# The same operations in an order searched over 48 replays with scattered landings in place of 16

## The chip, the cores and the metric

The kernel runs on one core of a Trainium2 chip. A core has five engines with a stream of instructions each: TensorE (PE in the profile; PEld is its weight loads), VectorE (DVE), ScalarE (ACT), GpSimd (POOL) and SyncE (SP), which here only issues transfers. POOL issues transfers too, the ones that add into their destination. The metric is device time in microseconds (us), less is better. Each engine works through its own stream in the order written, and the streams meet only at semaphores.

## The reference

For x of 2048 rows and 512 columns the reference computes

```
xn = layernorm(x)
q, k, v = split(xn @ wqkv)                  # 32 heads of 16
pq, pk = phi(q), phi(k)                     # phi(t) = (t + 1 if t > 0 else exp(t)) + 1e-6
o = pq @ (pk^T v) / (pq . sum(pk) + 1e-6)   # by head, no softmax
s = o @ wo
h = gelu(layernorm(xn) @ w1), its four column groups shifted by +1, -1, +2, -2 rows
x1 = xn + h @ w2
m = x1 + gelu(layernorm(x1) @ w3) @ w4      # 512 -> 1376 -> 512
out = x + s * silu(m)
```

## The kernel before

**Products.** Every float32 operand of a product is split into two pieces of the type fp32r, hi (a rounded copy, written by ACT or DVE) and lo (the residual full - hi, a DVE subtraction). A product is then three matmuls: hi by hi, hi by lo, lo by hi (`products`). In the tile names of the profile the last letter says which piece it is: `u_1h` and `u_1l` are the two pieces of `u_1`. Many products go by a scheme with seven block products for eight (`seven`, and `pair_kq` for keys and queries), in which a bank of PSUM takes a first product, is copied out by ACT, and then takes a second product on top.

**Stages in order of time.** Keys and queries of the 16 row tiles of 128 rows, with the gram matrix of x and the keys (`k`, `q`, `pax`, `pbx`, `pex`, `g` in the profile, 4 to 130 us); the row mixer with w1 and w2 (`h`, `pam`, `pbm`, `pem`, to 230); the MLP's first layer, block by block, with the attention products between (`pa`, `pb`, `pe`, `pas`, `pbs`, `pes`; for the first block also the second layer, `acc`, to about 405); the MLP's second layer of the other three blocks (`pad`, `pbd`, `ped`, to 492).

**The start.** Four 128-row chunks of the key weights (`wk_s0` to `wk_s3`) and of the transposed x (`xt0_0` to `xt0_3`, each in two halves) are loaded by SP in an order written out by hand. Four banks `k0` to `k3` take the keys of the first four row tiles, chunk by chunk; `k0` and `k1` take chunk 0 as plain float32 (`k<-wk_s,xt`). DVE sums the weights' chunks (`wkt`, three additions), a float32 product with ones (`ksum`) makes column sums of it, and `feature_k` turns a closed bank of keys into features: DVE `kt` (which needs ksum), ACT, DVE `kr`, ACT `k0h`. The first gram products (`g`) need `k0h` and the normalized x of the tile (`x0h`). The same sum for the query weights is `wqt` and `qsum`.

**What sets the order.** The body of the kernel issues nothing: it adds 5560 operations to a plan, each with its engine, an estimate of its duration and what it depends on. The operations are numbered in the order in which they are added. `Plan.emit` then runs a replay of the chip: again and again it takes, over all engines, the operation that can start first, and issues it, so that the order in which each engine's stream is written comes out of the replay. Among the operations of an engine that could start at about the same moment (within 0.02 us for PE, 0.25 us for the others) the one with the earliest due time goes. A PE operation's due time is its place in the list of matmuls; another operation's follows back from the matmuls that need it. A matmul may not run more than 9 us of products ahead of the first matmul still open (`window`). Products into one bank keep their order within that bank, since each depends on the one before it.

**The table.** Before the replay, `nudged` moves the due times of single operations by a table of pairs, number and k:

```
for n, k in zip(table[::2], table[1::2]):
    self.ops[n].due -= .25 * k
self.backward()
```

A positive k makes an operation due earlier by k quarters of a microsecond, a negative one later. `backward` then makes everything that is not a matmul due in time for those that need it, so a later due time of such an operation holds only where all of its users are later too. The loads of the start have due times 20 us apart in the order written by hand (`in_turn`), far ahead of all other.

Operations that the prediction speaks of, by number: 25 is the residual `u_1l` of the first half of chunk 1 (DVE); 26 the load of the first half of `xt0_2` (SP); 27 the copy `u_2h` of it (ACT); 98 the float32 product of chunk 0 into k1 (PE); 105 to 107 the three products of chunk 1 into k0 (106 is the one with `wk_1l`, 107 the one with `u_1l`); 108 to 110 the same into k1; 122 the last product into k1; 123 to 125 the additions of `wkt` (124 takes in `wk_s2`), 126 the product `ksum`; 174 the load of `wq_s0`; 3568 to 3573 the six products into the bank `pas` of the attention of row tiles 6 and 7; 3581 ACT's copy `p5s` of its bank `pes`; 3589 to 3594 the second product onto that bank.

Of the kernel before, what the change touches and what calls it, by code (L numbers as in the profile page):

```python
# [411 lines left out]
def linear_attn_gated_by_mixer(  # L412
# [1401 lines left out]
    for b in LINE:  # L1814
# [14 lines left out]
        25, 43, 34, 17, 48, 11, 52, 22, 57, 4, 63, 3, 76, 3, 88, -164, 90, 14, 91, -77, 94, 30, 95, 2, 96, 3,  # L1829
        97, 30, 98, -40, 100, -16, 103, 30, 105, -42, 112, 38, 115, -66, 118, -34, 124, 73, 125, 16, 129, 1,  # L1830
        147, 3, 150, 6, 151, -80, 176, 20, 207, 16, 216, 3, 233, 11, 234, 29, 248, 17, 252, 3, 259, 25, 261, 42,
        262, 18, 275, 8, 282, -131, 283, -49, 302, 83, 314, -14, 315, 24, 316, 21, 321, 25, 326, 6, 331, 17,
        336, -29, 341, -44, 354, 27, 355, -45, 375, 27, 405, -6, 406, -36, 410, -76, 415, 40, 416, -23, 424, 11,
        427, 23, 428, -30, 433, -9, 434, -77, 435, 22, 443, 67, 445, -24, 451, 7, 454, -24, 456, 18, 478, 13,
        485, -8, 488, -69, 489, -119, 491, -65, 492, -3, 504, 30, 522, 77, 532, -9, 542, -1, 544, 5, 545, 15,
        552, 36, 553, -28, 563, -29, 568, -26, 571, -22, 586, 29, 591, 24, 600, -25, 616, 11, 618, 10, 627, -50,
        631, 22, 650, 6, 654, -53, 657, -29, 660, 9, 676, 8, 678, 7, 688, -19, 694, -22, 704, -15, 705, 19, 710,
        -18, 713, 22, 714, 15, 717, -23, 721, -22, 724, 36, 726, -14, 728, 7, 733, 5, 761, 17, 797, 13, 806, 36,
        807, -10, 814, -15, 815, -38, 827, 85, 844, 20, 847, 3, 849, -51, 862, -35, 867, -36, 870, -19, 873, 31,
        874, -15, 876, -28, 885, 36, 894, 15, 899, 37, 901, -27, 909, 5, 911, 2, 917, 23, 925, 7, 927, -30, 934,  # L1840
        13, 941, -10, 956, -44, 969, 6, 971, -6, 976, -52, 980, -10, 997, 25, 998, -27, 1000, -24, 1005, -17,
        1013, -11, 1024, -19, 1030, -28, 1082, 6, 1087, -28, 1090, -3, 1101, 39, 1103, -27, 1119, 1, 1141, 13,
        1146, 44, 1149, 20, 1153, 9, 1156, 8, 1177, 27, 1179, 67, 1208, -23, 1213, 4, 1227, -38, 1239, -20,
        1262, 21, 1266, 8, 1271, 44, 1277, 35, 1291, 3, 1323, -12, 1324, -6, 1328, -1, 1329, 29, 1330, -16,
        1331, 19, 1333, -8, 1340, -40, 1362, -46, 1367, 18, 1381, 45, 1389, -46, 1399, -12, 1407, 24, 1408, 22,
        1412, 23, 1416, 13, 1419, 24, 1420, -43, 1421, -8, 1436, 8, 1447, 40, 1470, 42, 1474, -49, 1482, 33,
        1489, -12, 1502, -15, 1517, -42, 1521, -8, 1532, -28, 1540, -40, 1563, -18, 1575, 24, 1584, 20, 1588, 8,
        1596, -19, 1613, 37, 1614, 4, 1619, 33, 1620, 15, 1629, -4, 1631, -3, 1641, -35, 1648, 22, 1652, 49,
        1655, 4, 1659, 15, 1661, -4, 1665, -111, 1677, 11, 1679, -11, 1687, -19, 1696, 32, 1699, -20, 1700, 106,
        1703, -55, 1705, -12, 1717, -75, 1724, 10, 1725, 10, 1726, 15, 1741, 12, 1742, 28, 1747, 35, 1749, 12,  # L1850
        1758, 30, 1771, 17, 1779, -149, 1796, -30, 1843, 16, 1845, 18, 1853, -23, 1854, -28, 1855, -4, 1861,
        -22, 1864, 17, 1866, 31, 1881, -67, 1888, -54, 1901, 61, 1925, -37, 1933, -5, 1938, -86, 1943, 43, 1944,
        -6, 1947, 29, 1951, -16, 1955, -38, 1960, -57, 1964, 57, 1972, 19, 1978, 3, 1985, 4, 1990, -28, 1994,
        -42, 1996, -20, 1999, -38, 2000, 20, 2002, -22, 2008, 28, 2011, -25, 2021, 30, 2029, -31, 2048, -15,
        2049, -4, 2050, -3, 2060, 19, 2063, 43, 2067, 12, 2071, 19, 2080, 3, 2084, 22, 2102, 18, 2104, -26,
        2106, -32, 2112, -20, 2119, 24, 2131, -20, 2156, -24, 2158, 7, 2161, -34, 2190, -5, 2213, 12, 2244, 14,
        2258, 2, 2264, 71, 2267, 21, 2270, 19, 2286, -22, 2295, 5, 2298, -50, 2317, 33, 2326, 9, 2340, 14, 2353,
        12, 2357, 31, 2358, -19, 2381, -52, 2382, 1, 2383, 6, 2387, -14, 2389, -27, 2391, -30, 2393, -3, 2394,
        -15, 2406, 32, 2413, 22, 2422, -6, 2423, 26, 2424, -4, 2446, -16, 2452, 2, 2469, 9, 2471, 24, 2476, 31,
        2478, -18, 2482, 16, 2521, -26, 2534, -11, 2543, 24, 2578, -18, 2580, -14, 2585, 21, 2586, -7, 2592, -9,  # L1860
        2610, 16, 2611, 28, 2622, 21, 2626, 6, 2628, -27, 2639, 31, 2644, -22, 2648, 33, 2649, -8, 2656, -13,
        2658, 24, 2672, 29, 2684, -22, 2690, -4, 2691, -19, 2705, -23, 2710, 6, 2718, 6, 2722, -28, 2724, -47,
        2734, 26, 2739, 28, 2751, 44, 2778, 29, 2792, 17, 2804, 3, 2806, -46, 2816, -32, 2822, 20, 2831, -28,
        2833, 13, 2843, 6, 2855, 8, 2859, 52, 2870, 18, 2872, 8, 2875, 17, 2882, 33, 2892, -26, 2895, -23, 2899,
        -32, 2900, 16, 2904, -33, 2907, -13, 2912, 21, 2919, -24, 2926, 10, 2932, 4, 2935, -17, 2936, -40, 2941,
        -40, 2957, -40, 2963, -90, 2966, -48, 2967, -29, 2978, -20, 2980, 30, 2992, 14, 3029, -22, 3032, 9,
        3034, 36, 3055, 30, 3057, -6, 3061, -10, 3072, 62, 3085, 47, 3091, 25, 3094, 8, 3103, 7, 3124, 97, 3140,
        8, 3146, -6, 3156, -16, 3163, 24, 3204, 104, 3210, -44, 3222, -21, 3229, -63, 3239, -51, 3243, -24,
        3274, 55, 3276, 31, 3287, 41, 3288, 25, 3292, 22, 3311, -22, 3314, -18, 3315, -53, 3316, 21, 3319, -77,
        3321, -18, 3327, 2, 3328, -49, 3330, -52, 3347, 12, 3348, 25, 3374, 14, 3380, 18, 3386, 13, 3406, 28,  # L1870
        3407, -30, 3447, -19, 3450, 33, 3454, -46, 3458, 39, 3466, 50, 3469, -18, 3475, -27, 3480, 9, 3484, 35,
        3486, 106, 3490, -26, 3501, -40, 3509, 37, 3516, 10, 3541, 26, 3557, 4, 3559, 5, 3560, 3, 3561, 22,
        3562, 33, 3563, -30, 3570, 17, 3571, 56, 3584, -15, 3608, -28, 3611, 26, 3621, -42, 3626, 4, 3634, -6,
        3646, -38, 3669, 6, 3672, -26, 3676, -26, 3711, -20, 3721, 10, 3723, 5, 3739, 1, 3768, -3, 3776, 2,
        3777, 2, 3783, -4, 3791, -19, 3796, 7, 3813, -17, 3821, 23, 3826, -31, 3829, -38, 3846, -16, 3863, 11,
        3871, 6, 3878, 2, 3882, -23, 3885, -29, 3894, 61, 3897, -18, 3916, -7, 3926, -26, 3974, 6, 3987, 8,
# [59 lines left out]
```

## Time and profile before

| | |
|---|---|
| time, median of 3 runs | 498.06 us (498.03 to 498.6) |
| the profiled execution's own time | 498.08 us |
| its span, first to last instruction | 496.4 us |
| PE busy | 490.6 us, 99% of the span, 3244 instructions |
| PEld busy | 447.0 us, 90% |
| DVE busy | 438.4 us, 88% |
| ACT busy | 373.4 us, 75% |
| POOL busy | 123.6 us, 25% |
| granted TensorE clock, mean | 0.999 |
| moved by DMA | 117.44 MB, 237 GB/s |

A matmul instruction is on the row of PE from its start until its result is out, so rows of neighbouring matmuls overlap: what PE loses is read from the distance between starts, not from gaps between rows. A line of the timeline has the start, the time taken, engine, line, operation, out<-in, the shapes; in brackets the idle time before it and what ended that. A float32 product stands in the trace as two instructions (x2). SPq and POOLq are the queues that issue transfers.

### The profile page before, as it was taken

To read this page: it belongs to the slowest core of one execution; us is meant where nothing else is said; L and a number is where in the kernel's file an instruction comes from. 1 tells how busy PE (TensorE), PEld (TensorE's weight loads), DVE (VectorE), ACT (ScalarE), POOL (GpSimd) and SP (SyncE) were. 2 spreads that over 40 slices of the span, in tenths; PEclk is the share of its full clock that TensorE was granted. 3 is DMA by queue.
4 is the path that set the end of the run, shared out by engine and by line. 5 is a ranking of instruction groups with operands and counts; after the bars stand their busy time and mean duration, and the time that the engine had idled before them with its cause. 6 is when DMAs were issued, how large, how long until landed. Compare 5 with 4: busy or idle time off the path is not lost.

```text
span 496.4 us, 9885 instructions
## 1 busy us (share of the span) xinstructions
PE 490.6 (99%) x3244; PEld 447.0 (90%) x3244; DVE 438.4 (88%) x874; ACT 373.4 (75%) x845; POOL 123.6 (25%) x214
## 2 busy tenths in 40 slices
PE   8999999999999999999999999999999999999996
PEld 6778888888888999899889999999999999999996
DVE  5998997889989669999999999999999899796864
ACT  5999999677887599999988567765686877565531
POOL 1384404276930232133200021100000000143420
PEclk9999999999999999999999999999999999999999
DMA  7869696999974999999988499984634699599996
GB/s 229 303 187 297 133 296 183 237 287 269 329 220 100 236 310 248 273 252 290 337 268 247 158 194 298 247 262 138 183 114 147 215 336 332 114 226 283 278 224 182
DMA packets 87082, 117.44 MB, mean 237 GB/s; under 512 B 10328, under 2 KB 39160, under 8 KB 87032
## 3 DMA queue, kind: packets, MB, share of 16 engines
q1 hardware_dynamic: 75512, 96.11, 59.6%
q0 software_dynamic: 11520, 20.71, 24.9%
q8 instruction: 25, 0.41, 0.4%
q14 instruction: 25, 0.20, 0.1%
HBM read 72.66 MB, written 39.93 MB: 227 GB/s over the span
## 4 chain that ended last, share of the span: by engine, by line
PE 97%; DMA 1%; SPq 1%; ACT 0%; DVE 0%; issue 0%; ACTq 0%
PE pb L146 12%; PE pbd L146 9%; PE h L146 9%; PE g L146 9%; PE acc L146 6%; PE pe L146 6%; PE pbx L146 6%; PE ped L146 5%; PE pbm L146 5%; PE pbs L146 5%; PE q L146 3%; PE pa L146 3%; PE pex L146 3%; PE k L146 3%; PE pad L146 3%; PE pes L146 2%
## 5 line engine op out<-in xcount | busy, mean ns | idle before, releaser
L225 POOL DMA_DIRECT2D xo<-x1d x12 | 10.9, 950 | 166.2 <-DVE xo L191 118.5
L225 POOL DMA_DIRECT2D th<-in_x x14 | 12.2, 895 | 45.0 <-DVE th L201 23.1
L225 POOL DMA_DIRECT2D o<-xnd x16 | 14.0, 887 | 37.5 <-DVE o L191 13.5
L168 ACT ACTIVATE th<-xo 128x512 f32<-128x512 f32 (+1 forms) x16 | 9.7, 614 | 15.9 <-DVE xo L201 10.1
L225 POOL DMA_DIRECT2D zacc<-ke x12 | 12.9, 1073 | 31.4 <-DMA zacc<-ke 10.4
L191 DVE TENSOR_TENSOR ht<-h,abc 128x512 f32<-128x512 f32 x16 | 11.0, 690 | 7.5 <-PE h L146 7.4
L225 POOL DMA_DIRECT2D xt<-nrow x16 | 14.6, 1288 | 8.4 <-ACT k12h L168 4.1
L196 POOL TENSOR_SCALAR w<-mv 128x4 f32<-128x4 f32 (+2 forms) x10 | 2.5, 254 | 40.7 <-ACT sq L168 40.4
L168 ACT ACTIVATE y<-o,nm,rs 128x512 f32<-128x512 f32 x16 | 12.4, 814 | 0.2 <-POOL nm L196 0.2
L168 ACT ACTIVATE p<-pb 128x256 f32<-128x256 f32 x20 | 7.6, 381 | 5.8 <-PE pb L146 5.4
L168 ACT ACTIVATE ht<-ht 128x512 f32<-128x512 f32 x16 | 10.0, 626 | 2.1 <-DVE ht L191 2.0
L168 ACT ACTIVATE sq<-o,mv 128x512 f32<-128x512 f32 x16 | 11.5, 722 | 0.1
L168 ACT ACTIVATE u<-pb 128x256 f32<-128x256 f32 x20 | 7.7, 383 | 5.1 <-PE pb L146 4.5
L201 DVE SCALAR_TENSOR_TENSOR pq<-pq,rd 128x512 f32<-128x512 f32 x16 | 11.0, 688 | 0.3
L168 ACT ACTIVATE p<-pe 128x256 f32<-128x256 f32 x20 | 7.7, 384 | 4.6 <-PE pe L146 4.1
L201 DVE SCALAR_TENSOR_TENSOR qz<-pq,zb 128x512 f32<-128x512 f32 x16 | 10.8, 682 | 0.0
L1471 DVE TENSOR_REDUCE den<-qz 128x32 f32<-128x512 f32 x16 | 10.8, 679 | 0.0
L168 ACT ACTIVATE sq<-o 128x512 f32<-128x512 f32 x16 | 10.0, 629 | 0.1
L613 POOL TENSOR_TENSOR rs<-w,nhalf 128x4 f32<-128x4 f32 (+2 forms) x10 | 9.7, 970 | 0.8
L168 ACT ACTIVATE x<-x,nm,rs 128x512 f32<-128x512 f32 x12 | 9.2, 805 | 0.0
L201 DVE SCALAR_TENSOR_TENSOR th<-th,so 128x512 f32<-128x512 f32 x12 | 8.2, 683 | 0.6 <-ACT th L168 0.5
L168 ACT ACTIVATE sq<-x,mv 128x512 f32<-128x512 f32 x12 | 8.6, 718 | 0.1
(2075 smaller groups left out, 2446.9 us busy)
## 6 DMA issues: line engine op xcount, KB each, us to landing
w_s<-in_w SPq DMA_DIRECT2D x28, 256.0 KB, 5.6
x<-in_x SPq DMA_DIRECT2D x16, 256.0 KB, 6.2
xt<-in_xt SPq DMA_DIRECT2D x16, 256.0 KB, 6.9
xnd<-x SPq DMA_DIRECT2D x16, 256.0 KB, 5.9
xt<-nrow POOLq DMA_DIRECT2D x16, 256.0 KB, 7.6
pqd<-qr SPq DMA_DIRECT2D x16, 256.0 KB, 6.1
o<-xnd POOLq DMA_DIRECT2D x16, 256.0 KB, 6.6
x1d<-o SPq DMA_DIRECT2D x16, 256.0 KB, 5.1
```

What stands on the lines that cost most here:

```text
L146: lambda: nc.tensor.matmul(out.get(), lhs.get(), rhs.get(), start=start, stop=stop, skip_group_check=more))
L168: nc.scalar.activation(out.get(), src.get(), func, scale=get(scale), **kw)
L191: self.vec(eng, out, [a, b], lambda: self.e(eng).tensor_tensor(out.get(), a.get(), b.get(), op=op), True)
L196: lambda: self.e(eng).tensor_scalar(out.get(), a.get(), get(s1), get(s2), **kw), False,
L201: lambda: self.nc.vector.scalar_tensor_tensor(out.get(), a.get(), get(s), b.get(), op0=op0, op1=op1),
L225: lambda: self.nc.gpsimd.dma_start(out.get(), get(src), accum_op=ALU.add), mb=mb)
L613: lambda: g.tensor_tensor(out.get(), src.get(), nh.get(), op=ALU.pow))
L1471: pl.add("DVE", .6, .68, [t], [den], lambda: nc.vector.tensor_reduce(den.get(), t.get().rearrange("p (h d) -> p h d", d=DH), axis=AX.X, op ...
```

## The change

The table `SOONER` that `emit` gets is replaced by another one. Nothing else changes: the operations, their sizes, the tiles, the buffers and all the costs in the planner are the same. The old table has 666 pairs, the new one 732. 218 operations stand in both, 24 of them with the same value. By engine the old and the new table name: PE 431 and 458, DVE 109 and 129, ACT 66 and 63, SP 43 and 70, POOL 17 and 12. The core of the diff, the head of both tables:

```
     SOONER = (
-        25, 43, 34, 17, 48, 11, 52, 22, 57, 4, 63, 3, 76, 3, 88, -164, 90, 14, 91, -77, 94, 30, 95, 2, 96, 3,
-        97, 30, 98, -40, 100, -16, 103, 30, 105, -42, 112, 38, 115, -66, 118, -34, 124, 73, 125, 16, 129, 1,
-        147, 3, 150, 6, 151, -80, 176, 20, 207, 16, 216, 3, 233, 11, 234, 29, 248, 17, 252, 3, 259, 25, 261, 42,
...
-        3486, 106, 3490, -26, 3501, -40, 3509, 37, 3516, 10, 3541, 26, 3557, 4, 3559, 5, 3560, 3, 3561, 22,
-        3562, 33, 3563, -30, 3570, 17, 3571, 56, 3584, -15, 3608, -28, 3611, 26, 3621, -42, 3626, 4, 3634, -6,
...
+        26, -146, 27, -77, 28, -2, 46, -5, 48, -191, 56, 91, 66, 6, 79, 3, 88, -47, 91, -115, 95, 2, 96, 57,
+        100, -3, 102, 12, 106, -193, 111, -2, 112, -34, 113, -25, 119, -11, 122, -80, 124, 8, 142, -7, 151, -79,
+        156, -3, 166, 19, 171, 23, 174, 102, 176, 20, 181, 17, 185, 6, 188, 6, 193, 1, 229, 37, 232, 11, 248,
...
+        3497, 31, 3501, -33, 3505, 33, 3518, -53, 3541, 27, 3543, 13, 3560, 4, 3561, -14, 3568, -15, 3571, 53,
+        3594, -17, 3600, -10, 3605, -15, 3610, 36, 3615, -25, 3626, -14, 3627, -33, 3628, -32, 3634, -30, 3646,
...
     )
     pl.emit(first=6.0, lead={"p": 9.0, "w": 20.0, "ab": 10.0}, reserve={"p": 8, "w": 1, "ab": 0}, window=9.0,
             ahead=6.0, table=SOONER)
```

127 rows, old and new, of the table SOONER are left out of this document.

## The prediction

> **What bounds the kernel now.** The page first: who is busy, and what the chain of work that ended last consists of.
>
> ```profile
> PE 490.6 (99%) x3244; PEld 447.0 (90%) x3244; DVE 438.4 (88%) x874; ACT 373.4 (75%) x845; POOL 123.6 (25%) x214
> ...
> PE 97%; DMA 1%; SPq 1%; ACT 0%; DVE 0%; issue 0%; ACTq 0%
> ```
>
> The chain is TensorE from end to end, so an order can gain only where TensorE stands still. A busy share of 99% does not say where, because matmul rows overlap. I therefore take the distance between starts, from the chain in order of time, which merges unbroken runs of products:
>
> ```profile
> 35.05 4.64 PE g L146 x20
> ...
> 427.89 10.79 PE pbd L146 x91
> ```
>
> A 512-column product takes 4.64 / 20 = 0.232 us, a 256-column one 10.79 / 91 = 0.1186 us. Against these I hold the counts of two stages, from the view by stretches:
>
> ```profile
> 13.00:130.00 117.00, 117.00 (x506) 93.90 (x505) 104.34 (x191) 103.55 (x205) 58.29 (x109) 1.00 0.89 249
> ...
> 300.00:400.00 100.00, 99.93 (x842) 99.54 (x841) 96.13 (x206) 69.61 (x180) 2.60 (x3) 1.00 0.69 201
> ```
>
> 506 x 0.232 = 117.4 us fill the 117.0, and 842 x 0.1186 = 99.9 us the 100.0. Both stages are full to a few tenths. The list of waits agrees: TensorE has two, and the first lies ahead of all loads.
>
> ```profile
> PE warm L146 <- POOL ones L529: 1.1, 1, 1.1
> PE k L146 <- DVE u_1l L191: 0.4, 1, 0.4
> ```
>
> So all that a new order can win is a handful of places. I looked for them by the distance between starts. The largest is in the first 12 us, on the timeline of TensorE:
>
> ```profile
> 8.90 0.39 PE L146 MATMUL k<-wk_1l,u_1h 128*128 128x512 f32 x1
> ...
> 9.66 0.51 PE L146 MATMUL k<-wk_1h,u_1l 128*128 128x512 f32 x1 [0.37 <-DVE u_1l L191]
> ...
> 10.00 0.40 PE L146 MATMUL k<-wk_2h,u_2h 128*128 128x512 f32 x1
> ```
>
> From 8.90 to 10.00 two products take 1.10 us, where 0.46 would do: **0.63 us lost**, waiting for the residual u_1l. The second and third places are between 330 and 360 us:
>
> ```profile
> 338.15 0.39 ACT L168 ACTIVATE p5s<-pes 128x256 f32<-128x256 f32 x1 [1.16 <-PE pes L146]
> 338.24 0.28 PE L146 MATMUL pbs<-m_t2h,q6s0l 128*128 128x256 f32 x1
> ...
> 338.59 0.39 PE L146 MATMUL pes<-m_b22h,q6s1h 128*128 128x256 f32 x1
> 338.81 0.28 PE L146 MATMUL pes<-m_b22l,q6s1h 128*128 128x256 f32 x1
> ```
>
> ```profile
> 357.44 0.28 PE L146 MATMUL pe<-yt12h,w_s0h 128*128 128x256 f32 x1
> ...
> 357.97 0.39 PE L146 MATMUL pbs<-m_t4h,q 128*128 128x256 f32 x2
> ```
>
> 338.24 to 338.81 is 0.57 us for two products of 0.1186: **0.33 lost** while ACT copies the bank pes out before the second product may go onto it. 357.44 to 357.97 is 0.53 us for three: **0.17 lost**. Together 1.13 us, 0.23% of the time. What a measurement of this kernel can tell from no change is about 0.2%, 1.0 us; so even an order without a single one of these holes only just comes out as faster.
>
> The end does not give anything by itself: the last products run unbroken to the tail that follows from them.
>
> ```profile
> 489.81 2.27 PE pbd L146 x19
> 492.08 0.02 issue
> 492.10 0.39 ACT th L168
> ```
>
> **The change part by part.** No operation is added or removed, so the cost is in who waits for whom. I go through the places found above, then through what is moved elsewhere.
>
> *The hole at 9.1 us.* Who made u_1l late stands on the timeline of DVE and ACT:
>
> ```profile
> 7.36 0.41 ACT L168 ACTIVATE u_1h<-xt 128x256 fp32r<-128x256 f32 x1
> 7.49 0.69 DVE L191 TENSOR_TENSOR wk_1l<-wk_s,wk_1h 128x512 fp32r<-128x512 f32 x1
> ...
> 8.57 0.69 DVE L191 TENSOR_TENSOR wkt<-wkt,wk_s 128x512 f32<-128x512 f32 x1 [0.40 <-DMA wk_s<-in_wqkv]
> ...
> 9.04 0.41 ACT L168 ACTIVATE u_2h<-xt 128x256 fp32r<-128x256 f32 x1
> 9.18 0.42 DVE L191 TENSOR_TENSOR u_1l<-xt,u_1h 128x256 fp32r<-128x256 f32 x1
> ```
>
> u_1l's input was there at 7.77. It stood on DVE behind the sum wkt (operation 124), and that stood still for the landing of wk_s2. The old table has 124 due 73 quarters, 18.25 us, earlier; the new one 2.0 us. u_1l loses its own 10.75 us, but needs them no more: the products that use it (107, 110) come well ahead of the sum's (126) in the list. So u_1l should now follow wk_1l directly, at 8.2 in place of 9.18, done by 8.6, before TensorE asks for it at 9.14. That is worth the whole 0.63, if nothing else is late next. Two things can be.
>
> The first is u_2h. The load of its x (26) is due 36.5 us later; the loads of the start are 20 us apart, so it falls one place, behind wk_s3. At the rate of that stretch, 311 GB/s in the next row, 262 KB take 0.84 us; SP's issues are half a microsecond apart.
>
> ```profile
> 8.00:13.00 5.00, 4.63 (x17) 2.77 (x17) 4.57 (x12) 4.26 (x11) 0.66 (x2) 1.00 0.98 311
> ```
>
> u_2h, done at 9.45, would be done at 10.3 in place of being used at 10.00. The cover: wk_s3 comes earlier by the same step, so ksum (0.86 us of TensorE) may go in between. If it doesn't, 0.3 of the 0.63 comes back. Together with the next wait the bound is a gain of nothing.
>
> The second is x0h, at the first gram product:
>
> ```profile
> 18.33 0.62 ACT L168 ACTIVATE x0h<-x 128x512 fp32r<-128x512 f32 x1
> ```
>
> ```profile
> 19.00 0.19 PEld L146 LDWEIGHTS g<-k0h,x0h 128*128 128x128 f32 x1 [0.30 <-ACT x0h L168]
> ```
>
> ```profile
> 18.67 0.86 PE qsum L146 x2
> 19.53 2.79 PE g L146 x12
> ```
>
> The weight load waited for x0h until 19.00, unseen, because qsum kept TensorE busy until 19.53. With TensorE 0.63 earlier, qsum ends at 18.90; x0h is there at 18.95 to 19.00 if ACT's queue is what it was, and the load takes 0.19: the products begin at 19.19, which leaves 0.34 of the gain. I take **-0.35**, the nearer row; the ends are -0.63 (x0h earlier too) and 0.
>
> *The float32 product of k1* (98) is no longer held back 10 us and can run before 7 us. Products there are slower: the next rows show 0.34 us from start to start, then 0.24.
>
> ```profile
> 6.77 0.51 PE L146 MATMUL k<-wk_0l,u_0h 128*128 128x512 f32 x1
> 7.11 0.40 PE L146 MATMUL k<-wk_0h,u_0l 128*128 128x512 f32 x1
> 7.35 0.39 PE L146 MATMUL k<-wk_0l,u_0h 128*128 128x512 f32 x1
> ```
>
> I cost this at nothing: the slow stretch ends at a time, and what moves in pushes as much work out into the fast one. If the stretch went on because of it, it would cost up to its 0.86.
>
> *The hole at 338.6.* The new table makes the first product into pas (3568) due 3.75 us later, and its five others hang on it; these 6 x 0.1186 = 0.71 us are then left to run while ACT copies pes. That should close the 0.33.
>
> *458 matmuls are moved elsewhere.* The view shows no row for holes that do not exist yet. The nearest rows are the holes of the order of now: from nothing to as much as its largest, 0.63. The same rule of choice makes both orders, so I take as much anew as goes after 300 us, 0.33 + 0.17 with the second hole untouched by name: **0.0 net** after 300 us, ends -0.50 and +0.63.
>
> *The transfers.* 70 SP operations are moved (43 before), among them some twenty fetches of weights at 390 to 425 us, where DMA is full (share 1.04):
>
> ```profile
> 405.00:415.00 10.00, 10.00 (x87) 10.00 (x87) 9.95 (x21) 8.66 (x22) 0.00 (x0) 1.00 1.04 374
> ```
>
> ```profile
> 411.11 0.32 SPq L219 DMA_DIRECT2D wu_30l<-wt  x1
> ```
>
> ```profile
> L146 PE MATMUL ped<-wu_30l,d_s11h x6: 278/280/285, 421.0 to 480.9; 128*128 128x256 f32 x6
> ```
>
> This one is issued 9.9 us ahead of its first use. Fetches there are moved by 1 to 10 us in due time, and a place in the queue is about 0.6 us, so I cost them at nothing; without that lead, a transfer late by two places would cost 1.2.
>
> **Sum:** 498.08 (the profiled execution: span 496.4 and 1.68 around it) - 0.35 + 0.0 = 497.73; the median of the runs lies 0.02 lower. Forecast **497.7 us**, own range 498.08 - 0.63 - 0.50 = 496.95 to 498.08 + 0.63 = 498.7.
>
> **The rivals.**
>
> *All three holes close and none comes.* 498.06 - 1.13 = **496.9**. For it: the two larger ones are taken on by name. Against it: x0h must come earlier too, and the new order must be free of holes over 3,200 products, which the old one is not.
>
> *The hole only moves.* u_1l is early, u_2h late by as much, and k0's later close eats the rest: **498.1**. For it: the load order above. Against it: ksum can cover.
>
> *Slower: k0 closes too late.* 106 is due 48.25 us later, and the later products into k0 hang on it, so k1 to k3 may all go first. What follows is long:
>
> ```profile
> 13.67 0.74 DVE L201 SCALAR_TENSOR_TENSOR kt<-wneg,mv,k 128x512 f32<-128x512 f32 x1
> ...
> 21.19 0.68 DVE L191 TENSOR_TENSOR wq_0l<-wq_s,wq_0h 128x512 fp32r<-128x512 f32 x1
> ```
>
> ```profile
> 17.79 0.64 ACT L168 ACTIVATE k0h<-kr 128x512 fp32r<-128x512 f32 x1 [0.28 <-DVE kr L201]
> ```
>
> From kt to the end of k0h it is 18.43 - 13.67 = 4.8 us. With k0 closed last, at 18.7, there is no k0h before 23.4; TensorE has qsum until 19.5 and then nothing until the queries' second piece wq_0l is done at 21.87: 2.4 us lost, less 0.35, **500.1**. It decides once k0 closes more than about 0.5 us later than now, since k0h is 0.52 ahead of x0h. Against it: a late due time does not stop a product when nothing else can go, and the second halves of x were split only from 12.4 us on, so k0's products are what is left to run from 10 to 13 us.
>
> *The room is between the weight loads.* PEld is busy 447.0 of 496.4 us. If TensorE were free in the other 49.4 and an order used a tenth of it, that would be 4.9 us, **493.1**. Against it: in the stretch 13 to 130 the loads are busy 93.9 of 117.0, and 506 x 0.232 still fills it; the products themselves set the pace there. The Trainium skill ("Perfetto Trace Analysis", Identifying the Most-Contended Engine) says that headroom on TensorE is to be judged by the busy share of LDWEIGHTS and by flops, not by matmul busy time. By that rule there are 10% left; by the distance between starts, 0.2%, and here the trace does not agree with the rule.
>
> **How the numbers follow.** Forecast 0.46; the hole moves 0.20; all close 0.18; weight loads 0.02; k0 late, or another product late by over 1.3 us, 0.14. Faster by over 0.2% (under 497.06): 0.18 + 0.02 = 0.20. Slower by over 0.2% (over 499.06): 0.14. The rest, 0.66, is within. The range takes in the fast case and the upper end of the forecast, with half a microsecond of a beginning slow case: 496.7 to 499.2; outside it lie 0.02, most of the 0.14 and little else.
>
> **What would show it.** On the timeline of DVE u_1l directly behind wk_1l, near 8.2, and no wait of TensorE for u_1l; SP issuing wk_s3 ahead of xt0_2; the first g product at 19.1 to 19.3 in place of 19.53; products into pas between p5s and the second product onto pes near 338; 842 products, give or take three, from 300 to 400. I am wrong if TensorE's list of waits shows a new row over 0.5 us, if the first g comes after 19.6, or if the last product ends before 490.9 or after 493.1.

## The result, and the profile after

| | before | after |
|---|---|---|
| time, median | 498.04 us (497.94 to 498.6, 4 runs) | 501.13 us (500.17 to 501.57, 4 runs) |
| profiled execution: span | 496.4 us | 499.1 us |

The ratio is 1.0057, 95% interval 1.0040 to 1.0074: the new order is slower by 0.6%, some 3 us, and lies above the range of the forecast. The same order in two later series gave 1.0074 and 1.0069 (below).

The page of after: busy times hardly differ from those of before. The chain of work that ended last does: TensorE had 97% of it and now has 84%, and transfers have come into it.

```profile
PE 492.0 (99%) x3244; PEld 446.9 (90%) x3244; DVE 437.2 (88%) x874; ACT 374.4 (75%) x845; POOL 123.4 (25%) x214
...
PE 84%; DMA 8%; DVE 3%; ACT 2%; SPq 1%; POOL 1%; issue 1%; ACTq 0%; DVEq 0%; POOLq 0%
```

TensorE's list of waits in after had two rows in before, `warm` and `u_1l`:

```profile
PE warm L146 <- POOL ones L529: 1.1, 1, 1.1
PE pbm L146 <- ACT p1m L168: 0.6, 1, 0.6
PE g L146 <- ACT x0h L168: 0.4, 1, 0.4
PE ped L146 <- DVE d_s1xl L191: 0.3, 1, 0.3
PE k L146 <- DVE wk_1l L191: 0.3, 1, 0.3
PE pb L146 <- ACT p L168: 0.2, 1, 0.2
```

The view by stretches of after (stretch; length; busy time and count for PE, PEld, DVE, ACT, POOL; clock; DMA share; GB/s), then one stretch of before:

```profile
13.00:130.00 117.00, 116.61 (x502) 92.89 (x501) 103.24 (x190) 103.11 (x205) 57.81 (x109) 1.00 0.88 244
180.00:190.00 10.00, 9.40 (x78) 8.97 (x77) 5.84 (x14) 9.35 (x21) 3.14 (x5) 1.00 0.90 276
300.00:400.00 100.00, 99.94 (x837) 99.29 (x836) 96.05 (x205) 68.57 (x177) 3.45 (x4) 1.00 0.68 200
460.00:480.00 20.00, 19.65 (x167) 19.45 (x166) 15.29 (x31) 10.27 (x22) 5.94 (x8) 1.00 1.03 274
```

```profile
460.00:480.00 20.00, 20.00 (x171) 20.00 (x171) 16.23 (x33) 11.11 (x23) 7.32 (x10) 1.00 1.06 269
```

There are 502 products for 506 from 13 to 130 us, 837 for 842 from 300 to 400, 167 for 171 from 460 to 480: the loss is spread. The chain's last run of products and what follows:

```profile
492.56 2.37 PE pbd L146 x20
494.94 0.02 issue
```

That run ends at 494.93, where that of before ended at 492.08: 2.85 us later. Nothing of the difference lies in the tail behind it.

The change also touches the buffers, in a way that the section on the change does not have. Their number is the same, but the replay hands them out too, so another order puts tiles into other buffers: between the plans of the two kernels this holds for some 1,450 of the 1,650 tiles that have a numbered buffer.

By the distance between starts (each pause also makes the next product 0.10 us later than its own duration, which is left out here) the pauses of the new order are these, in after and in the two later executions of the same order, `order_again` and `order_third`:

| near | TensorE waits for | after | again | third |
|---|---|---|---|---|
| 9.2 us | wk_1l (DVE) | 0.49 | 0.49 | 0.39 |
| 19.5 | x0h (ACT) | 0.55 | 0.52 | 0.13 |
| 182 | p1m (ACT) | 0.72 | 0.86 | 0.99 |
| 184 | p5m (ACT) | 0.13 | 0.78 | 0.39 |
| 253 | p (ACT) | 0.33 | 0.32 | 0.32 |
| 340 | p5s (ACT), as in before | 0.22 | 0.22 | 0.22 |
| 470 | d_s1xl (DVE) | 0.51 | 0.70 | 1.68 |

The same places in all three, and at 19.5, 184 and 470 a size that changes from execution to execution.

### The profile page after: what moved, and what is told of

Its sections match the earlier page's. It is cut to its first block, busy times and chain, and to the rows that moved or that the text cites. A ratio compares the mean times of both kernels' runs of the same rounds, so it can differ in the third digit from the quotient of the medians.

```text
span 499.1 us, 9923 instructions
## 1 busy us (share of the span) xinstructions
PE 492.0 (99%) x3244; PEld 446.9 (90%) x3244; DVE 437.2 (88%) x874; ACT 374.4 (75%) x845; POOL 123.4 (25%) x214
## 4 chain that ended last, share of the span: by engine, by line
PE 84%; DMA 8%; DVE 3%; ACT 2%; SPq 1%; POOL 1%; issue 1%; ACTq 0%; DVEq 0%; POOLq 0%
PE pb L146 10%; PE g L146 9%; PE h L146 7%; PE pbd L146 7%; PE pbx L146 6%; PE pe L146 5%; PE pbs L146 5%; PE acc L146 4%; PE pbm L146 4%; PE q L146 3%; PE ped L146 3%; PE pex L146 3%; PE pad L146 3%; PE pa L146 2%; PE pes L146 2%; PE pem L146 2%
```

## How the experiments are built

A change of one due time shifts much of the replay behind it. So that a single operation can be moved, the order is written out: `emit` gets a list SEQUENCE of the 5560 numbers and issues exactly that (the core of the diff; the limits on how far a matmul may run ahead are switched off as well).

```
-    ahead=6.0, table=SOONER)
+    ahead=6.0, table=SOONER, sequence=SEQUENCE)
...
+            want = ops[sequence[len(done)]]
             for e, cands in avail.items():
                 picks = []
+                cands = [want] if want in cands else []
```

Each diff below shows one engine's part of that list, and the other engines' parts stay as they are. The buffers do not: the replay still hands them out, so a moved operation leaves many later tiles in other buffers, some 150 in copy_first, 230 in old_broken, 420 in one_move. No run separates the two. What can be said is that old_swap, old_start and old_moves, with some 165, 215 and 290 tiles in other buffers than before, cannot be told from before (1.0009, 0.9995 and 1.0004). All ratios are to the kernel before on the same chip in the same series. The theories at the start: **queue**, the loss lies where an engine's own order puts other work ahead of the copy that TensorE waits for; **landing**, it comes from transfers that land at other times in each execution; **give-back**, a pause that is closed comes back a little later.

| run | ratio | 95% interval | median, range (us) |
|---|---|---|---|
| order_again | 1.0074 | 1.0062 to 1.0086 | 502.2 (501.9 to 502.6) |
| order_third | 1.0069 | 1.0053 to 1.0085 | 502.2 (500.5 to 503.5) |
| one_move | 1.0074 | 1.0051 to 1.0097 | 501.9 (500.4 to 504.8) |
| three_moves | 1.0050 | 1.0029 to 1.0070 | 500.8 (499.2 to 505.0) |
| start_moves | 1.0052 | 1.0033 to 1.0071 | 501.3 (500.0 to 502.9) |
| landings_behind | 1.0050 | 1.0037 to 1.0063 | 501.3 (500.8 to 501.5) |
| all_moves | 1.0051 | 1.0039 to 1.0064 | 501.4 (500.7 to 501.5) |
| copy_first | 1.0041 | 1.0026 to 1.0055 | 500.0 (499.2 to 503.2) |
| copy_p1m | 1.0030 | 1.0020 to 1.0041 | 499.7 (499.0 to 501.7) |
| old_swap | 1.0009 | 0.9996 to 1.0021 | 498.8 (498.1 to 500.9) |
| old_broken | 1.0050 | 1.0034 to 1.0066 | 500.9 (498.8 to 503.4) |
| late_mended | 1.0042 | 1.0025 to 1.0058 | 500.9 (499.4 to 501.7) |
| both_mended | 1.0035 | 1.0023 to 1.0047 | 500.6 (499.6 to 501.0) |
| new_then_old | 1.0014 | 1.0006 to 1.0023 | 499.3 (498.5 to 500.0) |
| old_then_new | 1.0087 | 1.0074 to 1.0100 | 502.8 (502.3 to 503.9) |
| rest_mended | 1.0025 | 1.0016 to 1.0035 | 500.1 (499.7 to 500.7) |
| old_moves | 1.0004 | 0.9995 to 1.0013 | 498.7 (498.4 to 499.2) |
| old_start | 0.9995 | 0.9985 to 1.0006 | 498.5 (498.0 to 499.6) |

## The order or the execution

**order_again** and **order_third**: the new order, unchanged.

> The new order once more, with the sequence of all 5560 operations written out in place of the table; nothing else differs. Queue theory (the 2.7 us of span lie in five places where an engine's own order puts other work ahead of what TensorE waits for): the same median, 500.2 to 501.6, and another execution shows the pauses of TensorE at the same places, near 9.2 (0.5 us), 19.5 (0.55), 182 (0.7), 253 (0.3) and 470 (0.5). Landing theory (they come from transfers that land at other times in each execution): the same median, but at least two of the three late pauses gone from this execution and others in their place.

> The new order unchanged, once more, on the same chip as the three others: ratio 1.0057 to 1.0075, the pauses at 182, 184, 253 and 470 again, with 184 and 470 of another size than in the two executions seen so far.

The pauses stand in the table above: each at its place in all three executions. So the loss belongs to the order, with the buffers that go with it, against the landing theory; but the size varies threefold at 470, fourfold at 19.5 and sixfold at 184, against the queue theory alone. The median of order_again, 502.2, lies above the 500.2 to 501.6 that both theories had.

## One queue move at a time

**one_move**, ScalarE:

```
-  1436, 1632, 1567, 1663, 1568        # w4_1h, ht gelu, sq of o1, p1m, sq
+  1436, 1567, 1663, 1632, 1568
```

> The new order with one operation moved: on ScalarE the gelu into ht (1632) goes behind the copy p1m (1663), which then comes 0.6 to 0.8 us earlier near 181. Queue theory: the pauses at 181.9 and 184.2 (0.72 and 0.13, with 0.1 of slower restart each) close and the time falls by 0.8 to 1.0, to about 500.2, against the repeat of the new order. Give-back theory (the next wait behind it ends at the same moment): under 0.3 us, and a new pause within 5 us of the place. Landing theory: no change.

p1m came at 180.49 and its pause closed. The time did not move: 1.0074, as order_again in the same series. The waits of TensorE in this execution, and ScalarE's timeline:

```profile
PE pem L146 <- ACT p5m L168: 2.3, 1, 2.3
```

```profile
184.50 0.63 ACT L168 ACTIVATE sq<-o 128x512 f32<-128x512 f32 x1 [1.90 <-DMA o<-xnd]
185.03 0.19 ACT L168 ACTIVATION_READ_ACCUMULATOR sq<-o 128x1 f32 x1
185.12 0.36 ACT L168 ACTIVATE p5m<-pem 128x256 f32<-128x256 f32 x1
```

This is neither theory as first put. ScalarE stands still for 1.90 us until the accumulating load `o<-xnd` of tile 3 has landed, and behind the square that needs it stands p5m, for which TensorE waits. The order decides who stands behind the landing, the landing decides how long.

**three_moves**: the same, and on ScalarE p (2527) ahead of the third y; on VectorE:

```
-  5232, 5278, 5242, 5236              # d_s11l, dl1l, d_s21l, d_s1xl
+  5232, 5236, 5278, 5242
```

> The new order with three operations moved, one for each late pause: 1632 behind 1663 (ScalarE, 182 us), the copy p (2527) ahead of the third of three y copies (2215) (ScalarE, 253 us), the subtraction d_s1xl (5236) ahead of dl1l (5278) (VectorE, 470 us). Queue theory: 0.95 + 0.4 + 0.6 = 1.95 us less than the repeat, about 499.1. Give-back theory: about half of it, 500.1. Landing theory: 501.1 as before the moves.

The pauses at 182 and 470 are gone; the one at 253 is down from 0.33 to 0.15, but the sum of pauses from 240 to 260 us is about the same: that one is given back. That the one at 470 is gone says little for the move there, since it is gone in the executions of one_move, copy_first and copy_p1m too, in which nothing at 470 was moved: in one_move dl1h, for which d_s1xl waits in turn, found its transfer landed. 184 stood at 0.88 in this execution. 1.4 us less than the repeat in the medians, with a spread of 6 us, and the two intervals overlap.

**start_moves**, VectorE and ScalarE:

```
-  123, 25, 48, 124, 50, 28, 52, 31, 125 ... 128, 186, 187, 188, 131, 70
+  48, 25, 123, 124, 50, 28, 52, 125, 31 ... 128, 70, 186, 187, 188, 131
-  130, 184, 180, 132, 71
+  130, 71, 184, 180, 132
```

> The new order with the start alone mended: on VectorE wk_1l and u_1l ahead of the first sum wkt (48, 25, then 123), the last sum (125) ahead of the residual u_3l (31), x of tile 0 normalized right behind kt (70 behind 128), and on ScalarE its copy x0h (71) ahead of wq_3h (184). Queue theory: the pause at 9.2 shrinks from 0.59 to about 0.2 (u_2h is next, at 10.0) and that at 19.5 from 0.65 to 0.1 or less: 0.9 us less than the repeat, about 500.2. Give-back theory: the first gram product still starts after 19.2 and the time falls by under 0.3. Landing theory: the start's pauses vary by themselves by as much.

Both pauses closed, the weights' at 9 and x0h's at 19.5, and the ratio fell within its uncertainty. In the profiled execution a load of x landed late: u_0h ran at 6.36 in place of 4.65, and TensorE paused 1.14 us at 6.83; at 472 it paused 2.32 us for d_s1xl, the longest such pause of all the executions. Inconclusive on its size.

## What stands behind a landing

**landings_behind**:

```
-  1646, 1571, 1677, 1572              # ACT: ht gelu, sq of o3, p5m, sq of o3
+  1646, 1677, 1571, 1572
-  5177, 5277, 5241, 5201, 5250        # ACT: xo, dl1h, d_s21h, xo, d_s41h
+  5177, 5241, 5201, 5250, 5277
-  5232, 5278, 5242, 5236, 5251        # DVE: the same for dl1l
+  5232, 5242, 5236, 5251, 5278
```

> The new order with only the two instructions that wait for a transfer put behind the copies that TensorE waits for: on ScalarE the square of o3 (1571, which waits for the accumulating load of xnd) behind the copy p5m (1677); the pieces dl1h (5277, ScalarE) and dl1l (5278, VectorE), which wait for the load hl, behind d_s41h and d_s41l. Hostage theory (the copy stands behind an instruction that waits for a landing, and the landing comes 0.5 to 3 us later in one execution than in another): no pause over 0.2 us at 184 and at 470, whenever the transfers land; the ratio to the kernel before falls from 1.0074 by 0.6 to 2 us to about 1.004, and the runs lie closer together than the 2.4 to 4.4 us of the three last kernels. Queue theory as first put (p1m alone is what the order costs at 182): at most 0.6 less, from 470. Give-back theory: under 0.3, pauses of the same size within 5 us behind the two places.

p5m now ran at once, and TensorE's next wait at 184.67 was for u2m, which stands behind the same squares:

```profile
182.24 0.38 ACT L168 ACTIVATE p5m<-pem 128x256 f32<-128x256 f32 x1 [0.30 <-PE pem L146]
182.78 0.63 ACT L168 ACTIVATE sq<-o 128x512 f32<-128x512 f32 x1 [0.16 <-DMA o<-xnd]
...
184.25 0.36 ACT L168 ACTIVATE u2m<-pbm 128x256 f32<-128x256 f32 x1
```

Give-back, then, of 0.81 us at 184, and 1.0050 for the expected 1.004; the runs did lie closer together, within 0.8 us. The same happened at 470, and there the expectation had named the wrong transfer. ScalarE's and VectorE's timelines in after, and the chain of waits of after:

```profile
467.78 0.63 ACT L168 ACTIVATE dl1h<-hl 96x512 fp32r<-96x512 f32 x1 [1.38 <-DMA out<-th]
```

```profile
469.65 0.41 DVE L191 TENSOR_TENSOR d_s1xl<-d1f_s1xf,d_s1xh 128x256 fp32r<-128x256 f32 x1
```

```profile
458.11 9.59 DMA out<-th
```

dl1h needs only hl, yet it starts when the store `out<-th` has landed (458.11 + 9.59 = 467.70): what it has in common with th is the buffer that it takes over, by the plan that of the tile th10. In landings_behind and in late_mended, where dl1h goes later, the next in line, d_s11l, took that wait:

```profile
468.59 0.69 DVE L191 TENSOR_TENSOR d_s11l<-d1f_s11f,d_s11h 128x512 fp32r<-128x512 f32 x1 [2.44 <-DMA out<-th]
```

(late_mended; TensorE paused 0.88 us at 469.34 for it.) In before two things differ: SP issued this store at 452.52, 5.6 us earlier, and dl1h, at 464.10, sits in another buffer, that of a tile which VectorE reads last. Neither seems enough alone: in copy_p1m dl1h takes over th10's buffer too, the store goes out at 455.06, and dl1h does not wait. So at 470 the new order costs by the buffer that it hands out together with the late store, not by the place in a queue alone.

**all_moves**: landings_behind with the start's moves, 1632, 2527, and the six products into pas (3568 to 3573) directly ahead of the second product onto pes.

> The new order with all repairs together: the start's five, p1m ahead of the gelu, p ahead of the third y, the two instructions that wait for landings put behind, and the six products into pas (3568 to 3573) directly ahead of the second product onto pes (3589). Hostage theory: what the new order costs is these places and nothing else, so it comes down to the kernel before or a little under it: ratio 0.998 to 1.001, 497.5 to 499. Give-back theory: half of the 3.7 us stay, ratio about 1.004. Another cause, not in these places (products that run slower, transfers that slow each other): above 1.005.

1.0051: the sum of the repairs did not add up. Its waits of TensorE say why:

```profile
PE pbm L146 <- ACT u2m L168: 1.5, 1, 1.5
...
PE pes L146 <- DVE q6s0l L191: 0.3, 1, 0.3
```

The landing is handed on to u2m, and the pas products, taken from their place, uncovered another wait, for q6s0l (a pause of 0.50 at 340.2 where the old one was 0.22).

## Where the landing becomes late

So the question is why the load of o3 comes late at all. ScalarE and POOL's queue, before:

```profile
173.82 0.38 ACT L168 ACTIVATE o<-pbm 128x256 f32<-128x256 f32 x1 [2.78 <-PE pbm L146]
174.10 0.63 ACT L168 ACTIVATE sq<-o 128x512 f32<-128x512 f32 x1
```

```profile
174.50 0.86 POOL L225 DMA_DIRECT2D o<-xnd  x1 [2.88 <-PE h L146]
```

And after:

```profile
173.26 0.63 ACT L168 ACTIVATE sq<-o 128x512 f32<-128x512 f32 x1 [1.37 <-DMA o<-xnd]
...
175.37 0.63 ACT L168 ACTIVATE sq<-o 128x512 f32<-128x512 f32 x1 [1.39 <-DVE ht L191]
175.91 0.19 ACT L168 ACTIVATION_READ_ACCUMULATOR sq<-o 128x1 f32 x1
176.00 0.36 ACT L168 ACTIVATE o<-pbm 128x256 f32<-128x256 f32 x1
```

```profile
173.35 0.28 PE L146 MATMUL pbm<-w_t4h,ha220l 128*128 128x256 f32 x1
```

```profile
176.66 0.89 POOL L225 DMA_DIRECT2D o<-xnd  x1 [3.14 <-ACT o L168]
```

TensorE closes the bank at 173.8 in before and at 173.6 in after. In before the copy into o3 goes out at once; in after it stands behind the squares of o0 and o2 and runs at 176.00. The first of these waited 1.37 us for a transfer into o0, the second 1.39 us. The row names `ht` of VectorE, which ended in the same 0.1 us, but by its dependencies the second square needs the transfer into o2, and it was that: the last completion of this load is at 175.30 in the trace, 0.07 us ahead of the square. In landings_behind it is at 174.17, and the square starts at 174.24, where the row names another operation of VectorE and `ht` still runs until 174.96:

```profile
174.24 0.63 ACT L168 ACTIVATE sq<-o 128x512 f32<-128x512 f32 x1 [1.30 <-DVE hs3f L191]
```

So the copy stood behind two landings. The load that adds into o3 is issued 2.2 us later (176.66 for 174.50), so its squares wait (by 0.08 us in after, 0.33 in order_third, 0.71 in order_again, 1.90 in one_move), so p5m and u2m behind these are late: what holds up one copy delays the next landing. The Trainium skill ("PSUM — Partial Sum Buffer", Engine vs sequencer instructions) states that the queues of ScalarE, VectorE and GpSimdE are strictly first in, first out; the trace agrees, with the 2.4 us that the copy stood behind. The Trainium skill ("DMA: Bandwidth & Descriptors", Anatomy of one DMA) has about 2.0 us and the bytes at 436 GB/s for a transfer issued by GpSimd, which would be an estimated 2.6 us for these 262 KB. The trace does not agree: here they took 6.5 to 7.7 us from issue to the square that waited for them, beside a DMA share of 0.90.

**copy_first**, ScalarE, one move in the new order; **copy_p1m**, the same and the move of one_move:

```
-  1416, 1510, 1514, 1565, 1511        # hs21h, sq of o0, sq of o2, copy into o3, sq
+  1416, 1565, 1510, 1514, 1511
```

> The new order with one operation moved: on ScalarE the copy of bank pbm into o3 (1565) ahead of the two squares (1510, 1514) that wait for the landings of o0 and o2, as the order of before has it. Chain theory (copy behind a landing, so the load it feeds is issued 2.2 us later, so the squares of o3 wait, so p5m and u2m behind them are late for TensorE): the copy runs near 174.1 in place of 176.0, the load o<-xnd is issued near 174.5 in place of 176.7, ScalarE does not wait for it at 183, the pause at 184 falls to 0.25 or less in whatever execution, and the ratio falls from 1.0074 to 1.003 to 1.005; the pauses at 182, 253 and 470 stay. Give-back theory: ratio above 1.005.

> The new order with two moves: the copy into o3 ahead of the squares (as in the run copy_first), and the gelu behind p1m (as in one_move). Chain theory: no pause over 0.25 us between 180 and 190, since the landing of o3 no longer stands behind it: 0.5 to 0.9 us less than copy_first, ratio 1.002 to 1.0035. Give-back theory: the pause comes back at pem or pbm within 5 us and the ratio stays at 1.004.

In copy_first the copy runs at 173.82 and the load goes out at 174.50:

```profile
173.82 0.39 ACT L168 ACTIVATE o<-pbm 128x256 f32<-128x256 f32 x1 [1.77 <-PE pbm L146]
```

```profile
174.50 0.89 POOL L225 DMA_DIRECT2D o<-xnd  x1 [0.83 <-ACT o L168]
```

No pause at 184 is left, and the one move takes the ratio from 1.0069 or 1.0074 to 1.0041. The interval, 1.0026 to 1.0055, lies below that of order_again, but it touches that of order_third and overlaps that of the first series, 1.0040 to 1.0074. With p1m ahead of the gelu as well it is 1.0030 (1.0020 to 1.0041), below order_again and order_third, and from 180 to 200 us TensorE pauses no more than in before: with the load early, p1m's pause no longer comes back at p5m, as it did in one_move. Both as the chain theory had them, but for the pause at 470, which was to stay and is in neither execution.

**old_swap** and **old_broken**: the order of before with the places of after put in, on ScalarE.

```
-  1431, 1677, 1571                    # both: w4_5h, p5m, sq of o3
+  1431, 1571, 1677
-  1416, 1565, 1510, 1514              # old_broken too
+  1416, 1510, 1514, 1565
```

> The order of before with one change taken from the new order: on ScalarE the square of o3 (1571, waits for the accumulating load of xnd) ahead of the copy p5m (1677) in place of behind it. Hostage theory: p5m comes 1.1 us later than at 181.48 at least, TensorE pauses at the second product onto pem near 182.7 by 0.3 to 2 us, and the time rises by 0.4 to 1.5 us over the kernel before with a wider spread. Give-back theory: no change beyond 0.2 us, as TensorE has kv products to fill in.

> The order of before with two changes on ScalarE taken from the new order: the copy into o3 (1565) behind the two squares (1510, 1514), and the square of o3 (1571) ahead of p5m (1677). Chain theory: the load o<-xnd is issued some 2 us later than at 174.50, ScalarE waits for it at 182 to 184, TensorE pauses at pem or pbm there by 0.3 to 2.5 us: ratio 1.001 to 1.004 and runs spread over 2 us or more. Give-back theory: no change, ratio under 1.001.

The swap of p5m alone cannot be told from nothing (-0.2 to 1.0 us), where the expectation had 0.4 to 1.5: with the load issued at 174.41 it has landed in time. With the copy behind the squares as well, the kernel before becomes 0.5% slower, 2.5 us (1.7 to 3.3), more than the 1.001 to 1.004 expected, and its runs scatter from 498.8 to 503.4. ScalarE in its profiled execution, which was its fastest:

```profile
182.06 0.63 ACT L168 ACTIVATE sq<-o 128x512 f32<-128x512 f32 x1 [0.86 <-DMA o<-xnd]
...
182.69 0.36 ACT L168 ACTIVATE p5m<-pem 128x256 f32<-128x256 f32 x1
```

TensorE paused 0.59 us at 183.11 for that p5m. So two places of ScalarE's stream, with the buffers that come with them, are enough for most of the loss. How they make it is shown for a small part only: this execution is 0.35 us above the median of before. Of the slower ones there is no profile; that they are longer by later landings is inferred from one_move, where the pause was 2.48 us. In this execution both squares ahead of the copy waited for transfers (1.62 and 0.81 us).

## The rest

**late_mended** (the repairs after 170 us together, with p5m moved as in landings_behind) and **both_mended** (with the start's as well):

> The new order with that move and those for the other late places (p1m ahead of the gelu, p5m ahead of the square of o3, p ahead of the third y, dl1h and dl1l behind the pieces wanted sooner); start and pas as the new order has them. Chain theory: no pause over 0.25 us after 20 us; what is left over the order of before is the start's 0.25 to 0.6 and some 0.4 of small pauses from 300 to 360: ratio 1.001 to 1.0025, and runs within 1.5 us of each other. Give-back theory: above 1.004.

> The same with the start's five moves too. Chain theory: ratio 1.000 to 1.002. If the start's moves only move its pause (as the order of before showed when u_1l was put first): the same as without them, within 0.3 us.

1.0042 and 1.0035, both above what was expected. Their profiles show pauses of 0.54 us at pbm near 184 to 185 for u2m, which copy_first without the move of p5m does not have: that move is a loss in itself, as landings_behind had shown and I had not yet drawn from it.

**new_then_old** and **old_then_new**: the two orders spliced.

> Each engine works in the new order up to about 110 us, the rest in the order of before. Chain theory: only the start's share of the loss is left, 0.25 to 0.6 us: ratio 1.0005 to 1.0015. If the start carries the open rest: 1.003 or more.

> The order of before up to about 215 us, the new order from there. Chain theory: the pauses at 253 (0.4 us), 300 to 360 (0.4 us more than before) and 470 (0.5 to 2 us, by the landing of hl) are left, those at 182 to 185 are gone: 1.4 to 2.5 us, ratio 1.002 to 1.004 (these are what is left open). If the new order's late part costs only what its three late pauses show without the landing: 1.0015. If all of the loss lies before 215 us: under 1.001.

The new order up to 110 us costs 0.14%, 0.7 us (0.3 to 1.2). The other splice, 1.0087 for an expected 1.002 to 1.004, says nothing on size: at its seam, between 184 and 220 us, it has pauses of its own of 2.0 us together, which neither order has. Its late pauses are those of the new order: 0.31 at 254.6, 0.72 at 471.6.

**rest_mended**: copy_p1m with the start's five moves and d_s1xl ahead of dl1l.

> The new order with the copy into o3 ahead of the squares, the gelu behind p1m (as copy_p1m), the start's five moves (as start_moves) and d_s1xl ahead of dl1l (as three_moves); p5m, p and pas as the new order has them. If these places are the loss: no pause at 182 to 185 and at 470, and of the 1.0030 of copy_p1m the start's 0.0014 and some 0.0005 for 470 go: ratio 1.0005 to 1.002, with the pause at 252 (0.4 us) and some 0.3 us between 280 and 360 left. If the ratio stays at 1.003: what is left lies in places that the profile does not show as pauses.

1.0025, just above the expected 1.0005 to 1.002, and the runs lie within 1.0 us of each other, where those of copy_first spread over 4.0. TensorE's waits have one row left that before has not:

```profile
PE pb L146 <- ACT p L168: 0.2, 1, 0.2
```

The last product of this execution ends 1.5 us later than that of before (493.6 for 492.1). By the distances between starts 0.4 of it lies from 240 to 260 us (that wait), some 0.2 each from 300 to 360 and from 20 to 40, the rest in smaller pieces. For these 0.25% no single cause was found, and I did not take them apart.

## The holes of before

**old_moves** and **old_start**: the order of before with its start changed (25 ahead of 124; 70 and 71 right behind kt), old_moves with the pas products moved too.

> The order of before with its own three holes worked on: on VectorE u_1l (25) ahead of the second sum wkt (124), x of tile 0 normalized right behind kt (70) and its copy x0h (71) ahead of the scaling of kt (180), and the six products into pas directly ahead of the second product onto pes (3589). If the holes of before are worth what the distances between starts say: 0.5 to 0.95 less, ratio 0.998 to 0.999, 497.1 to 497.6. Give-back theory: no change. The third hole, near 357, stays.

> The order of before with only the start changed: u_1l (25) ahead of the second sum wkt (124), x of tile 0 and its copy x0h right behind kt (70, 71); pas untouched. If the hole of 0.63 us at 9 us is worth its size: ratio 0.9987 to 0.9993. If it only moves on to u_2h at 9.6 to 10 (as in old_moves, where that pause was 0.87 us): 0.9995 to 1.0008. The pause at 338 stays as it was (0.22), where old_moves made 0.57 of it.

Neither is faster. In old_moves u_1l came early and TensorE paused 0.87 us at 9.59 for u_2h instead; moving pas made 0.57 of the 0.22 at 338. In old_start the products from 8.44 to 11 us follow each other without a pause of 0.1 us, and the execution lost 1.0 us ahead of it, where a load of x was late:

```profile
6.01 0.42 ACT L168 ACTIVATE u_0h<-xt 128x256 fp32r<-128x256 f32 x1 [2.29 <-DMA xt<-in_xt]
```

So there is no version here that beats the kernel before.

## Why the prediction was wrong

**What bounds the kernel.** That TensorE fills its stages but for a few places was right for before. It made me price the change by TensorE's holes, and the loss of the new order arises on ScalarE and on the queues, and only arrives at TensorE.

**The hole at 9.1 us.** u_1l did come at 8.16, for the forecast 8.2, and SP issued wk_s3 earlier, as written. But the time was met by chance: u_1l came ahead of wk_1l, not behind it. VectorE in after:

```profile
8.16 0.43 DVE L191 TENSOR_TENSOR u_1l<-xt,u_1h 128x256 fp32r<-128x256 f32 x1 [0.28 <-ACT u_1h L168]
8.51 0.68 DVE L191 TENSOR_TENSOR wk_1l<-wk_s,wk_1h 128x512 fp32r<-128x512 f32 x1
```

The new table makes wk_1l (48) due 47.75 us later; the entry stands in the diff as quoted, and I read 124 and 25 beside it and not it. So the hole only moved, the rival at 498.1, by another operation than the one named there. Of closing it alone, old_start shows no gain that can be measured.

**The float32 product of k1** ran from 6.04 us, and from its start to that of the second row behind it took 1.09 us, as in before (7.81 to 8.90): to cost it at nothing was right.

**x0h.** The step held that the g products would start at 19.19, kept by x0h. x0h was 0.5 us later still, since kt started at 14.29 for 13.67, because the last sum wkt was 1.5 us later (11.59 for 10.12) behind the residuals. From kt on that is the way of the rival "k0 closes too late", at a quarter of its size; but kt waited for the sum and not for the bank, whose last product started at 13.05 for 12.93. The 12 g products of the chain end at 22.59 for 22.32. new_then_old puts the start's whole loss at 0.7 us; the step had -0.35.

```profile
19.51 3.08 PE g L146 x12
```

**The hole at 338** stayed (0.22 at 340.55): 3568's later due time did not move its products. The runs in which they were moved show that they already covered a wait for q6s0l, so the 0.33 was not to be had that way.

**458 matmuls moved elsewhere, 0.0 net: this is the step that failed.** It took one hole of the size of the largest as the upper end, for all places together, set new against gone, and counted only what lies after 300 us; the stages from 20 to 300 us, where the pauses at 182, 184 and 253 arose, got no term at all. In place of 0.0 the runs showed 2.5 us (1.7 to 3.3) when the copy 1565 and the copy 1677 were put behind squares in the order of before, and next to nothing for 1677 alone. Two more things were wrong in it. It counted the matmuls that the table names, while of the operations that cost, 1510, 1514, 1565, 1571, 1632 and 1663 stand in neither table; 1677 stands in both, and came behind 1571 although the new table makes it due 7.5 us earlier, the old one 2.75. They change places because the replay does: of the matmuls 72% are followed by the same matmul as before, of ScalarE's operations 31%, of VectorE's 31%, of SP's 42%. And the price of a changed place was taken from pauses that TensorE had, while the price of a copy behind a square goes by the time of a landing, for which the page of before had 6.6 us for these transfers on POOL's queue.

**The transfers cost nothing** was wrong too, not for the fetches of weights of which it spoke, but for the stores `out<-th`: later by 5.6 us on SP, the first of them kept until 467.7 a buffer that dl1h does not have in before, and TensorE paused 0.51 to 1.68 us at 470 in the three executions of the unchanged order.

**The rival "another product late by over 1.3 us"** was nearest in time (500.1), but as one wait. What came are several of 0.1 to 1.7 us. **The room between the weight loads**: PEld's busy time is the same (446.9 for 447.0) with the time 3 us longer; nothing here speaks for it.

**What was to show me wrong** did: a new row of 0.6 us in the list of waits (p1m), and the last product ends at 494.9, after 493.1. From 300 to 400 us there are 837 products, outside 842 give or take three.

## What to carry to other kernels

When the order of an engine's stream changes, look in each stream for an instruction that waits for a transfer, or for a buffer, and ask what stands right behind it: a copy that frees a bank, or one that feeds the next transfer, can be worth more than its own 0.4 us, since it is then late by a landing. Before a pause is closed by a move, look at who waits behind the same landing next; here that handed the pause on in five of the runs, and putting the transfer itself earlier did not. A planned order holds as a whole: the entries of a table that name an operation say little about which operations change places, and where buffers are handed out in the order of issue, they change with it.

## What the runs showed of the hardware that I had not expected

The same load, issued at the same time, lands at quite different times. The second half of the first chunk of the transposed x is issued at 2.18 us in all executions, and u_0h, which waits for it, started between 4.65 and 5.20 in 16 of 20 profiled executions and at 5.47, 6.01, 6.29 and 6.36 in four. The accumulating load of o3, issued within 0.2 us of the same time, took 6.5 us in after (176.66 to 183.13) and 7.7 us in one_move (176.77 to 184.50) up to the square that waited for it.

A wait of TensorE costs more than itself: the product behind the one that waited starts 0.22 us after it in place of 0.1186, at every pause of the 256-column products that I looked at.

```profile
181.88 0.39 PE L146 MATMUL pbm<-w_t2h,hs21h 128*128 128x256 f32 x1 [0.60 <-ACT p1m L168]
182.10 0.28 PE L146 MATMUL pbm<-w_t2l,hs21h 128*128 128x256 f32 x1
```
